# Softmax factors of three chunks spread by VectorE instead of by DMA, and a fold ahead of an accumulate, in a fused attention and expert kernel

## The chip, the cores and the metric

The kernel runs on one core of a Trainium2 chip. The metric is the device time of one execution in microseconds (us). PE is TensorE, DVE is VectorE, ACT is ScalarE, POOL is GpSimd, and SP is the engine that issues most DMAs. A `q` behind a name (SPq, POOLq) is that engine's instruction queue.

## The reference

For one sequence of S = 2048 tokens and D = 1024 channels, two branches over the same input are mixed by a gate. Their core:

```python
qkv = (x @ wqkv).reshape(B, S, 3, 32, 32).transpose(2, 0, 3, 1, 4)
scores = einsum("bhqd,bhkd->bhqk", q, k) * 32 ** -0.5
o = einsum("bhqk,bhkd->bhqd", softmax(scores), v)
a = o.transpose(0, 2, 1, 3).reshape(B, S, D) @ wo
# b: per head h a top-1 choice out of 64 experts, out = sum_h gelu(x . u[e]) * v[e]
g = sigmoid((x * gate_w).sum(-1))
out = g * a + (1 - g) * b
```

The change concerns attention's last stage alone: the row sums of the softmax and the product with `wo`.

## The kernel before, in words

**Attention.** The 32 heads run one after the other, each over NT = 16 key tiles of 128. For a tile, TensorE computes scores (L1292), ScalarE exponentiates them into a tile `P[h, kt]` of 128x2048 (L1301), and TensorE multiplies them with the values into `o` (L1313). The softmax is not normalized there. Its denominators, the sums of `P` over keys, are gathered beside it: VectorE adds the tiles of a head into `ACC[h]` (`presum`, `add_pair`, `merge`, all through `add`, L1353, two instructions of 128x1024 for a tile), and some pairs of tiles are first added by DMAs that accumulate, issued by POOL (`accumulate`, L1342). `pairs_of(h)` names the pairs as (target, source). For the last head, 31, they are (2, 4) and (2, 6): both add into `P[31, 2]`.

**Row sums.** For most heads, DMAs on POOL's queue fold `ACC[h]` from 128 partitions to 64 and to 32 (`fold`, L1361), store them (`store_rows`, tensors `sed`), and later fold these in DRAM. For the last group (heads 28 to 31) TensorE does the end of it: head 30's `ACC` is folded to 64 partitions, `rows_back` (L1373) loads the stored rows of heads 28 and 29 into its other half, and `rowsums` (L1326) multiplies head 31's last two tiles, `ACC[31]` and `ACC[30]` by ones. `norm_sums` copies the sums out (ScalarE, tile `ssb`) and stores them in `smd`; `load_r` reads them back as `rr`, `norm_r` takes VectorE's reciprocals, and the result goes to the tensor `rd`: one factor for each head and token.

**What sets the order there.** A dictionary `todo` of steps, one step for a key tile. `at(step, f, ...)` puts a call in a step; the calls of one step run in the order in which the loop over heads entered them. Each engine's queue runs in program order. An issued DMA waits for the landing of the eighth one before it that was issued on the same side (POOL, or SP and ACT), as they share eight semaphores.

**Output.** The result is computed in eight chunks of W = 256 tokens. For chunk n, `load_o` loads `OC[n]` (tile `V`, eight DMAs of 128x256 from the tensors `od`) and `load_rb` the factors `RB[n]`: a factor belongs to a head, which is 32 partitions of `OC`, so a row of `rd` is loaded 32 times, once into each of the 32 partitions, by a DMA whose source repeats. Four such DMAs (j = 0 to 3) make a chunk. VectorE multiplies `OC[n]` by `RB[n]` in two halves of 128x1024. Chunks 0 and 1 go through `split_o` (each operand split into a high and a low part, L1627) and plain matmuls (`wo_mm`, L1559, three products of 128x512 for a block); `av_mm` (L1566) adds the expert branch with the operand `at`. Chunks 2 to 7 go through `scale_o` (L1612) and a Strassen scheme: `ht.operand(...)` forms A11, S3, S1 and so on from `OC[n]`, `ht.product("P1")` and so on runs twelve matmuls each (L155). The last head's group (kc = 7) can be normalized only when the row sums are there; so chunks 0 and 1 load their rows 0 to 6 ahead and row 7 later. `RB[0]` lies in `rb0`, and `RB[n]` in a tile `P8` or `P9`.

TensorE runs `wo_mm` of chunk 0 over kc 0 to 6, `av_mm` of chunk 0, `wo_mm` of chunk 1 over 1, 2, 3 and 0, then chunk 0's kc 7, chunk 1's kc 4 to 6, `av_mm` of chunk 1 and its kc 7, and then chunk 2's P1, P7, P5, P6 and so on.

## Time and profile before

| | |
|---|---|
| median of 3 runs | 1811.92 us (1811.81 to 1812.72) |
| profiled execution | 1813.99 us, its span 1812.2 us |
| PE busy | 1798.1 us, 99% of the span |
| DVE busy | 1495.0 us, 82% |
| ACT busy | 1216.4 us, 67% |
| POOL busy | 281.6 us, 16% |
| granted TensorE clock, mean | 0.998 |
| DMA | 362.19 MB, mean 200 GB/s |

The span is the time from the first to the last instruction of one profiled execution. Busy times of different engines overlap. In the 14 us in which PE isn't busy lie its start and the end of the kernel too. The attention stage ends near 1620 us of the span, and the output stage fills the rest.

### The profile page before, as it was taken

What the parts mean: (1) busy time and instruction counts of PE and PEld (TensorE: products, weight loads), DVE (VectorE), ACT (ScalarE), POOL (GpSimd) and SP (SyncE); (2) the same over time, 40 slices, a digit from 0 to 9 for tenths busy, and PEclk for the clock granted to TensorE, in tenths of its full rate; (3) what the DMA queues carried; (4) which work ended last, traced back from release to release, by engine and by line L of the source; (5) the groups of instructions that cost most, each with busy time, mean ns of one, the idle gap of its engine ahead of it and who ended that gap; (6) DMA issues with size and microseconds to landing.
All of it is one profiled execution on the core that took longest, in us unless ns stands there. A gap on an engine that the chain in (4) does not pass through costs nothing.

```text
span 1812.2 us, 27968 instructions
## 1 busy us (share of the span) xinstructions
PE 1798.1 (99%) x10559; PEld 1136.5 (63%) x10559; DVE 1495.0 (82%) x1673; ACT 1216.4 (67%) x1604; POOL 281.6 (16%) x351
## 2 busy tenths in 40 slices
PE   9999999999999999999999999999999999999899
PEld 7877777788888745554555545455555455448787
DVE  6868776358987689899899899999989989893684
ACT  4434321211233399999999999999999999982221
POOL 0212000026401211111111111111121111221000
PEclk9999999999999999999999999999999999999999
DMA  6887889823238688899899998998999998977861
GB/s 234 242 283 241 273 272 292 262 79 106 82 130 273 228 199 182 175 187 193 185 207 188 208 195 181 193 211 193 198 216 200 207 214 189 203 172 183 283 177 59
DMA packets 132050, 362.19 MB, mean 200 GB/s; under 512 B 18676, under 2 KB 57732, under 8 KB 106360
## 3 DMA queue, kind: packets, MB, share of 16 engines
q0 software_dynamic: 22736, 134.89, 36.6%
q1 hardware_dynamic: 89016, 189.56, 36.1%
q10 hardware_dynamic: 20160, 35.92, 7.0%
q8 instruction: 84, 1.38, 0.3%
q14 instruction: 54, 0.44, 0.1%
HBM read 176.77 MB, written 86.61 MB: 145 GB/s over the span
## 4 chain that ended last, share of the span: by engine, by line
PE 90%; DMA 4%; ACT 2%; DVE 1%; SPq 1%; issue 1%; POOL 0%; ACTq 0%; DVEq 0%; POOLq 0%
PE ring L1292 27%; PE o L1313 25%; PE bk L155 11%; PE bk L711 9%; PE pa L155 6%; PE bk L758 5%; PE bk L926 2%; PE bk L311 2%; PE bk L491 1%; ACT P L1301 1%; SPq L82 1%; DMA wraw<-in_wqkv 1%; DMA V<-od 1%; PE bk L395 1%; PE pa L1566 1%
## 5 line engine op out<-in xcount | busy, mean ns | idle before, releaser
L1301 ACT ACTIVATE P<-ring 128x512 f32<-128x512 f32 (+3 forms) x986 | 808.1, 942 | 14.0 <-PE ring L1292 8.5
L1353 DVE TENSOR_TENSOR acc<-acc,P 128x1024 f32<-128x1024 f32 x408 | 469.4, 1215 | 22.1 <-ACT P L1301 22.1
L1313 PE MATMUL o<-P,V 128*32 128x512 f32 (+1 forms) x4040 | 412.6, 529 | 0.0
L1292 PE MATMUL ring<-Q,K 98*128 98x512 f32 x1024 | 268.5, 406 | 0.1
L1292 PE MATMUL ring<-z,z 98*128 98x512 f32 x1020 | 267.6, 406 | 0.1
L1292 PEld LDWEIGHTS ring<-Q,K 98*128 98x128 f32 x1024 | 182.6, 188 | 116.8 <-ACT P L1301 38.6
L1292 PEld LDWEIGHTS ring<-z,z 98*128 98x128 f32 x1020 | 182.1, 188 | 114.6 <-issue 37.8
L1313 PEld LDWEIGHTS o<-P,V 128*32 128x32 f32 x4040 | 111.6, 109 | 218.2 <-issue 198.4
L1353 DVE TENSOR_TENSOR rb<-rb,P 128x1024 f32<-128x1024 f32 x186 | 214.3, 1215 | 5.6 <-ACT P L1301 5.6
L1342 POOL DMA_DIRECT2D P<-P x60 | 55.7, 928 | 362.9 <-PE o L1313 141.8
L240 ACT ACTIVATE hi<-bk 128x512 fp32r<-128x512 f32 x40 | 23.7, 595 | 111.5 <-PE bk L711 94.7
L1301 ACT ACTIVATE wo_raw<-ring 128x512 f32<-128x512 f32 (+3 forms) x115 | 97.5, 942 | 0.7
L711 PE MATMUL bk<-xh,e 128*128 128x512 f32 x384 | 94.5, 394 | 0.2 <-DVE e L101 0.2
L711 PE MATMUL bk<-xl,e 128*128 128x512 f32 x384 | 92.2, 389 | 0.0
L711 PEld LDWEIGHTS bk<-xh,e 128*128 128x128 f32 x384 | 70.9, 188 | 22.5 <-issue 3.4
L711 PEld LDWEIGHTS bk<-xl,e 128*128 128x128 f32 x384 | 72.1, 188 | 15.0
L253 DVE TENSOR_TENSOR lo<-bk,hi 128x512 fp32r<-128x512 f32 x40 | 27.6, 689 | 64.8 <-ACT hi L240 59.7
L101 DVE TENSOR_TENSOR e<-wraw,e 128x512 fp32r<-128x512 f32 (+3 forms) x64 | 54.3, 858 | 29.7 <-ACT e L100 29.0
L1301 ACT ACTIVATE vhl<-ring 128x512 f32<-128x512 f32 (+3 forms) x89 | 76.9, 939 | 0.9 <-PE ring L1292 0.2
L100 ACT ACTIVATE e<-wraw 128x512 fp32r<-128x512 f32 (+3 forms) x64 | 44.7, 705 | 42.6 <-DMA wraw<-in_wqkv 26.1
L1353 DVE TENSOR_TENSOR acc<-acc,wo_raw 128x1024 f32<-128x1024 f32 x60 | 70.1, 1216 | 1.8 <-ACT wo_raw L1301 1.8
L155 PE MATMUL bk<-xh,e 128*128 128x512 f32 x288 | 68.6, 393 | 0.0
(305 smaller groups left out, 2454.7 us busy)
## 6 DMA issues: line engine op xcount, KB each, us to landing
P<-P POOLq DMA_DIRECT2D x60, 1024.0 KB, 10.2
wqt<-in_wq SPq DMA_DIRECT2D x26, 1024.0 KB
wraw<-in_wqkv SPq DMA_DIRECT2D x30, 512.0 KB
acc<-acc POOLq DMA_DIRECT2D x21, 512.0 KB, 6.6
qdh<-hi ACTq DMA_DIRECT2D x32, 256.0 KB
qdl<-lo ACTq DMA_DIRECT2D x32, 256.0 KB
kdh<-hi ACTq DMA_DIRECT2D x32, 256.0 KB
kdl<-lo ACTq DMA_DIRECT2D x32, 256.0 KB
```

The lines of the kernel that those rows point to most:

```text
L100: nc.scalar.activation(hi, src, AF.Copy)
L101: (on or nc.vector).tensor_tensor(out=lo, in0=src, in1=hi.bitcast(F32), op=OP.subtract)
L155: nc.tensor.matmul(ps, self.a[a][i][:, k, :], self.b[b][j][k], start=(not first and k == 0 and i == j == 0), stop=(k == HC - 1 and i == 1))
L311: nc.tensor.matmul(ps[32 * quad:32 * quad + 32, :], kpad[:, quad % 2, i, :], t[:, quad, :], start=(i == 0), stop=(i == 3))
L711: nc.tensor.matmul(ps, t[:, kc // HC, a, kc % HC], x_at(b, n, kc), start=first, stop=last)
L758: nc.tensor.matmul(ps, x_at(a, t // 4, kc)[:, tok], b, start=first, stop=last)
L926: nc.tensor.matmul(p, x_at(a, t // 4, kc)[:, tok], b, start=first, stop=last)
L1292: on_ring(nc.tensor.matmul(ring[:, i, :], K[:98, kt * 128:(kt + 1) * 128], Q[:98, qc * 512:(qc + 1) * 512], start=True, stop=True), i)
L1301: on_ring(nc.scalar.activation(P[h, kt][:, q0 * 512:(q0 + m) * 512].rearrange("p (a m) -> p a m", a=m), ring[:, i:i + m, :], AF.Exp, scale ...
L1313: nc.tensor.matmul(O[h][32 * qc:32 * qc + 32, c0:c1], Vt[g][:, kt, 32 * j:32 * j + 32], p[:, qc * 512 + c0:qc * 512 + c1], start=(kt == 0) ...
L1342: nc.gpsimd.dma_start(P[h, b], P[h, a], accum_op=OP.add)
L1353: nc.vector.tensor_add(out[:, c], a[:, c], b[:, c])
```

## The change

Four edits, all at the end of attention and in the output stage.

1. `norm_sums` stores the four heads' sums with one DMA of 16 rows instead of four DMAs of 4 rows.
2. An `accumulate` runs at step a + 2 instead of b + 4. For every pair with a = b + 2 that is the same step. Only head 31's second pair, (2, 6), moves, by two steps, and comes behind the fold of head 30, which was entered in that step before it.
3. For chunks 1 to 3, `load_rb` loads a row into the first of its 32 partitions only. POOL sets the tile to zero first (`memset`, 128x2048), and `factors` has VectorE's shuffle copy partition 0 of each 32 to all 32, in place, ahead of each product. Chunk 3 reuses chunk 1's tile.
4. In the program's order, rows 0 to 6 of chunk 1's factors come ahead of its `V` loads, those of chunk 2 right behind them (on POOL's queue, before on SP's), and chunk 3's factors move from POOL's queue to SP's, behind chunk 0's output.

```diff
     def norm_sums(ps):
...
-        for j in range(4):
-            dma(SMD[G - 1][j:j + 1, :].rearrange("o (q s) -> (o q) s", q=NQ), o[8 * j::32, :])
+        dma(SMD[G - 1].rearrange("j (q s) -> q j s", q=NQ), o[::8, :])
...
+    SHUFFLED = 1, 2, 3
...
     def load_rb(n, k0, k1, js=range(4), queue=nc.sync):
-        if n not in RB:
+        if n == 3:
+            RB[n] = RB[1]
+        elif n not in RB:
             RB[n] = rb0 if n == 0 else wk.tile([128, KC, W], F32, name=f"P{8 + n % 2}", bufs=1)
+            if n in SHUFFLED:
+                nc.gpsimd.memset(RB[n], 0.0)
+        rows = 1 if n in SHUFFLED else 32
         for j in js:
             src = RD[k0:k1, j:j + 1, n * W:(n + 1) * W].rearrange("g j s -> j g s")
-            dma(RB[n][32 * j:32 * j + 32, k0:k1, :], src.to_broadcast([32, k1 - k0, W]), queue)
+            dma(RB[n][32 * j:32 * j + rows, k0:k1, :], src.to_broadcast([rows, k1 - k0, W]), queue)
+
+    def factors(n, k0, k1):
+        r = RB[n][:, k0:k1, :]
+        if n in SHUFFLED:
+            flat = r.rearrange("p k m -> p (k m)")
+            nc.vector.stream_shuffle(flat, flat, [0] * 32)
+        return r
...
         for b, a in pairs_of(h):
-            at(base + b + 4, accumulate, h, b, a)
+            at(base + a + 2, accumulate, h, b, a)
...
         for k in range(2):
             o = OC[n][:, k * HC:(k + 1) * HC]
-            nc.vector.tensor_mul(o, o, RB[n][:, k * HC:(k + 1) * HC])
+            nc.vector.tensor_mul(o, o, factors(n, k * HC, (k + 1) * HC))
...
     def split_o(n, k0, k1):
         o = OC[n][:, k0:k1, :]
-        nc.vector.tensor_mul(o, o, RB[n][:, k0:k1, :])
+        nc.vector.tensor_mul(o, o, factors(n, k0, k1))
...
-    load_chunk(1, 0, KC - 1, nc.gpsimd)
+    load_rb(1, 0, KC - 1, queue=nc.gpsimd)
+    load_o(1, 0, KC - 1, nc.gpsimd)
+    load_rb(2, 0, KC - 1, queue=nc.gpsimd)
...
-    load_rb(2, 0, KC)
+    load_rb(2, KC - 1, KC)
     load_o(2, 0, KC)
...
     split_o(1, HC, KC)
-    load_rb(3, 0, KC, queue=nc.gpsimd)
     load_at(2)
...
     plain_out(0, pa, nc.gpsimd)
+    load_rb(3, 0, KC)
     load_o(3, 0, KC)
```

What that does to the queues is best seen in three places. First POOL's queue around head 30's fold, before the change. `P_12653` is `P[31, 2]`, `P_12687` and `P_12722` are its two sources, `acc<-acc` is head 30's fold, `acc<-sed` the two loads of `rows_back`, and `V` is chunk 1's:

```order
L1342 DMA P_12653<-P_12687 128x2048
L1342 DMA P_12653<-P_12722 128x2048
L1361 DMA acc<-acc 64x2048
L1373 DMA acc<-sed_95 32x2048 x2
L82 DMA V<-od_71 128x256
```

After the change, with `P_12961` for the factors of chunk 1:

```order
L1342 DMA P_12653<-P_12687 128x2048
L1361 DMA acc<-acc 64x2048
L1342 DMA P_12653<-P_12722 128x2048
L1373 DMA acc<-sed_95 32x2048 x2
L1421 MEMSET P_12961 128x2048
L82 DMA P_12961<-rd 1x7x256 x4
L82 DMA V<-od_71 128x256
```

The fold has passed the second accumulate, and a memset and four loads of a few rows stand ahead of `V`. Second, further down in POOL's queue, from chunk 1's last `V` load to the stores of chunk 0, before (`P_12969` are chunk 1's factors, `P_13216` chunk 3's):

```order
L82 DMA V<-od_77 128x256
L82 DMA P_12969<-rd 32x7x256 x4
L82 DMA at<-atd 128x256 x2
L82 DMA P_13216<-rd 32x8x256 x4
L82 DMA out<-rb_5214 128x512 x4
```

And after (`P_12975` are chunk 2's):

```order
L82 DMA V<-od_77 128x256
L1421 MEMSET P_12975 128x2048
L82 DMA P_12975<-rd 1x7x256 x4
L82 DMA at<-atd 128x256 x2
L82 DMA out<-rb_5214 128x512 x4
```

A second memset stands ahead of `at`, and chunk 3's factors have left the queue. Third, VectorE from the reciprocals to chunk 2's operands, before (`V<-V,P` are the products with the factors, `rr` the row sums, `pa` the results of chunk 0):

```order
L1402 RECIPROCAL rr<-rr 128x64
L1403 TENSOR_TENSOR rr<-rr,G_110 128x64
L1627 TENSOR_TENSOR V<-V,P_12969 128x1024
L101 TENSOR_TENSOR acc<-V,z_13110 128x1024
L1627 TENSOR_TENSOR V<-V,rb_5214 128x256
L101 TENSOR_TENSOR acc<-V,z_12763 128x256
L1627 TENSOR_TENSOR V<-V,P_12969 128x1024
L101 TENSOR_TENSOR acc<-V,z_13110 128x1024
L1622 COPY rb_5214<-pa_12922 128x512
L1622 COPY rb_5214<-pa_12924 128x512
L1612 TENSOR_TENSOR V<-V,P_13115 128x1024 x2
```

And after:

```order
L1402 TENSOR_TENSOR rr<-rr,G_110 128x64
L1431 STREAM_SHUFFLE P_12961<-P_12961 128x1024
L1639 TENSOR_TENSOR V<-V,P_12961 128x1024
L101 TENSOR_TENSOR acc<-V,z_13114 128x1024
L1639 TENSOR_TENSOR V<-V,rb_5214 128x256
L101 TENSOR_TENSOR acc<-V,z_12762 128x256
L1431 STREAM_SHUFFLE P_12961<-P_12961 128x1024
L1639 TENSOR_TENSOR V<-V,P_12961 128x1024
L101 TENSOR_TENSOR acc<-V,z_13114 128x1024
L1634 COPY rb_5214<-pa_12922 128x512
L1634 COPY rb_5214<-pa_12924 128x512
L1431 STREAM_SHUFFLE P_12975<-P_12975 128x1024
```

Each product with the factors of chunks 1 to 3 has a shuffle right ahead of it. TensorE's and ScalarE's own sequences are the same as before.

## The prediction

> **What bounds the kernel now.** I read the engine totals first, then the stages, then TensorE's own timeline, and only then the chain of waits. TensorE is busy nearly throughout (the table above), so the only time to be had is where it stands still or runs slowly. The timeline of TensorE's instructions from 1600 us on (start, busy time, line, count, idle time before with its releaser in brackets) shows two such places:

> ```profile
> 1624.88 2.07 PE L1326 MATMUL o<-acc,ones 128*32 128x512 f32 x8
> 1629.05 1.06 PE L1326 MATMUL o<-acc,ones 128*32 128x512 f32 x8 [2.09 <-DMA acc<-sed]
> 1630.05 2.05 PE L1559 MATMUL pa<-woh,z 128*128 128x512 f32 x4
> ...
> 1634.49 1.07 PE L1559 MATMUL pa<-woh,z 128*128 128x512 f32 x4
> ...
> 1648.09 1.98 PE L1566 MATMUL pa<-vhl,at 128*128 128x512 f32 x8
> ...
> 1675.29 1.07 PE L1559 MATMUL pa<-woh,acc 128*128 128x512 f32 x4
> 1681.10 0.64 PE L155 MATMUL pa<-woh,acc 128*128 128x512 f32 x1 [4.74 <-ACT acc L100]
> ...
> 1685.85 0.40 PE L155 MATMUL pa<-z,s 128*128 128x512 f32 x1
> ```

> Gap A: the row sums of head 30 wait 2.09 us for `rows_back`. Gap B: the first Strassen product of chunk 2 waits 4.74 us for its operand A11. Each gap has a tail in which TensorE runs at about half clock. The table of stages (length, busy time of PE, PEld, DVE, ACT, POOL, then granted clock, DMA share, GB/s) shows the clock after each gap, and that nothing like it follows:

> ```profile
> 1630.00:1632.00 2.00, 2.00 (x9) 1.57 (x6) 0.68 (x3) 1.81 (x4) 1.70 (x3) 0.53 0.99 403
> 1682.00:1684.00 2.00, 1.82 (x5) 1.36 (x5) 1.30 (x3) 0.63 (x1) 0.00 (x0) 0.50 0.98 409
> 1690.00:1812.00 122.00, 118.43 (x523) 97.73 (x521) 79.14 (x118) 25.05 (x42) 0.00 (x0) 1.00 0.54 152
> ```

> From 1690 us the 122.00 us hold 118.43 us of matmul, and the rest is the final store: whatever brings TensorE earlier to 1690 us brings the end earlier by as much.

> What the gaps are worth: at full clock twelve wide matmuls take 2.72 us (four start every 0.907 us). From 1630.05 to 1634.49 there are twelve, which took 4.44, so gap A costs 2.09 + 1.72 = 3.81 us. Gap B starts where the last four should end, 1675.29 + 0.91 = 1676.20; the product starts at 1681.10 (4.90 later) and its twelve matmuls last until 1685.85 (4.75, 2.03 too long): 6.93 us. Both together are 10.74 us, the most that this change can bring.

> [...]

> **The fold ahead of the second pair.** POOL's queue and the chain of waits behind it:

> ```profile
> 1598.61 0.90 POOL L1342 DMA_DIRECT2D P<-P  x1 [4.28 <-ACT P L1301]
> 1609.07 0.88 POOL L1342 DMA_DIRECT2D P<-P  x1 [9.56 <-ACT P L1301]
> 1609.62 1.18 POOL L1361 DMA_DIRECT2D acc<-acc  x1
> 1622.47 0.51 POOL L1373 DMA_DIRECT2D acc<-sed  x1 [1.39 <-DMA rb<-rd]
> 1632.83 0.59 POOL L82 DMA_DIRECT2D at<-atd  x1 [0.90 <-DMA V<-od]
> ```
> ```profile
> 1609.62 10.66 DMA acc<-acc
> 1622.47 6.54 DMA acc<-sed
> 1632.43 10.06 DMA smd<-ssb
> 1670.15 10.29 DMA V<-od
> ```
> ```profile
> 1595.74 9.16 DVE L1353 TENSOR_TENSOR acc<-acc,P 128x1024 f32<-128x1024 f32 x8
> 1604.82 0.41 DVE L1441 TENSOR_TENSOR V<-V,ssb 128x256 f32<-128x256 f32 x1
> 1616.69 9.16 DVE L1353 TENSOR_TENSOR acc<-acc,P 128x1024 f32<-128x1024 f32 x8
> 1679.16 2.54 DVE L1612 TENSOR_TENSOR V<-V,P 128x1024 f32<-128x1024 f32 x2 [14.84 <-DMA V<-od]
> ```

> The second accumulate adds into the same tile as the first, so it can't go before the first has landed; the ScalarE named there had long written the tile. The fold stands behind it although its own input, head 30's merge, is the last of the eight additions that end at 1604.82. Ahead of it, the fold goes at about 1604.9 instead of 1609.62, 4.7 us earlier. With the same 10.66 and 6.54 us to landing, `rows_back` lands at 1629.01 - 4.7 = 1624.3. Late next is head 31's own sum: its additions end at 1616.69 + 9.16 = 1625.85, and TensorE is through with them at 1626.95. So 2.7 us are to spare and gap A goes whole. The accumulate put behind loses nothing, as it waits for the first one's landing anyway; with the fold's 10.66 us to landing it ends at 1619.7, and VectorE's third addition, which reads it, is due at 1616.69 + 2 x 2.29 = 1621.27.

> **The loads, the shuffles, the one store.** Sizes per DMA and time to landing (KB each, us), then three lines of the timelines of ScalarE and SP:

> ```profile
> P<-rd SPq DMA_DIRECT2D x4, 256.0 KB
> P<-rd POOLq DMA_DIRECT2D x4, 256.0 KB, 13.6
> P<-rd POOLq DMA_DIRECT2D x4, 224.0 KB, 8.9
> V<-od POOLq DMA_DIRECT2D x7, 128.0 KB, 7.1
> out<-rb POOLq DMA_DIRECT2D x4, 256.0 KB, 13.1
> 1647.00 1.06 ACT L100 ACTIVATE z<-V 128x1024 fp32r<-128x1024 f32 x1 [9.18 <-DVE V L1627]
> 1630.81 2.10 SPq L82 DMA_DIRECT2D smd<-ssb  x4
> 1657.84 13.37 SPq L82 DMA_DIRECT2D V<-od  x8
> ```

> The factors of chunks 1 to 3 are 0.9 + 1 + 1 MB, and become a thirty-second of that. Three 0.5 us issues of `smd` fall away (1.6 us). So the chain row sums, `smd`, `rr`, reciprocal, `rd` moves by at least 2.1 + 1.6 = 3.7 us, and by more if `smd`'s 10.06 us shrink, since the 0.9 MB of chunk 1 were moving just then. In it stands one new shuffle. TensorE needs the operand behind it after the eight matmuls of 1648.09, at 1649.9 - 3.81 = 1646.1. ScalarE's half of it ended at 1648.06, so 1648.06 - 3.7 + 1.2 = 1645.6: no wait even without any gain in the DMA.

> Gap B hangs on chunk 2's eight `V<-od`: issued from 1657.84, landed at 1670.15 + 10.29 = 1680.44, 22.6 us for 1 MB, with 2 MB of factors (SP's ahead of them, POOL's beside) and 1 MB of stores in flight. TensorE will be ready at 1676.20 - 3.81 = 1672.4. The products and A11's rounding took 1681.10 - 1680.44 = 0.7 us past the landing and the low half 1.9, so the data must land by 1670.4. Bounds: nothing gained, 22.6 us, lands at 1657.84 - 3.7 + 1.2 + 22.6 = 1677.9; issue at 0.4 us each and the 6.54 us of `rows_back`, about 10, lands at 1665. Without 2 of 4 MB I take the half, 11.3 us: 1666.6, nearly 4 us to spare. One third less is enough to hide it all. Gap B goes whole.

> The shuffle is not in this trace. Nearest is the product of the same 128x1024 form, 2.54/2 = 1.27 us; the dearest VectorE form is this reciprocal:

> ```profile
> 1644.95 0.55 DVE L1402 RECIPROCAL rr<-rr 128x64 f32<-128x64 f32 x1 [4.28 <-DMA rr<-smd]
> L1812 POOL MEMSET const-float32-0.0<- 128x1 f32 x1 | 0.1, 100 | 0.3 <-issue 0.3
> L137 POOL TENSOR_TENSOR wraw<-wraw,wraw 128x512 f32<-128x512 f32 x5 | 8.1, 1616 | 0.4
> DMA to landing us min/median/max: 8.2/8.4/8.7
> ```

> At its pace 1024 columns would be 8.8 us, the upper end; no gain is possible, as each is one more instruction. I take 1.2, six of them, 7.2 us. [...] Chunk 1's two are covered above, chunk 2's by the 4 us to spare (the first needs no `V`), chunk 3's two by VectorE being busy 79.14 of 122.00 us while TensorE holds eight banks of products. Uncovered they would cost 2.5 us a chunk. Chunk 3's factors move from POOL to SP ahead of its `V` loads, four small issues whose reader is one product group later: nothing.

> The two memsets of 128x2048 stand in POOL's queue ahead of chunk 1's loads and of `at`, TensorE's operand at 1648.09 - 3.81 = 1644.3. Bounds: 0.1 us (a 128x1 memset) and 4 x 1.62 = 6.5 us (adding two inputs); one written, none read, I take 2.6. The first waits for the second accumulate and `rows_back`, about 1619. Fifteen issues of 0.59 us follow before `at` goes, at 1619 + 8.9 + 5.2 = 1633.1, about as now (1632.83). Each issue also waits for the landing of the eighth before it, `at` for the fourth `V`: that one goes at 1619 + 2.6 + 8 x 0.59 = 1626.3 and lands 7.1 later, 1633.4, which is no more. `at` lands 8.4 later at 1641.8. With 2.5 us to spare, memsets up to 3.8 us cost nothing.

> **The sum.** 3.81 + 6.93 = 10.74 us off the profiled execution, 1813.99 - 10.74 = 1803.25. The median of the runs, 1811.92, is 2.07 under that execution. If the 2.07 lay outside the gaps the median becomes 1801.2; if they lay within the gaps, 1803.2. I take the middle, 1802.2.

> **The rivals.**
> *Only gap A goes.* `V` of chunk 2 lands at 1677.9 at worst, five and a half us after TensorE is ready, and gap B stays as long as it was: 1811.92 - 3.8 = 1808.1. For it: each `V` issue waits for an earlier landing, and 1 MB of stores stays. Against: two thirds of what went before and beside them is gone. Chance of this or something between it and the forecast 0.13, spread over 1803.4 to 1808.

> *Only gap B goes.* The early fold shares the DMA engines with the first accumulate, or `rows_back` with the second, and 2.7 us to spare are eaten: 1811.92 - 6.9 = 1805.0. Against: the same bytes in the same stretch. Chance 0.06.

> *The change doesn't do what it says*: the waits move on to the same length (a `T` block or `rr` late instead), 1811 to 1812. Chance 0.03.

> *Slower: the memset.* If a memset of 2048 columns takes far longer than an addition does, chunk 1's loads and `at` are late. At 6.5 us each `at` goes at 1640.9 and lands at 1649.3, 5.0 after need; with 1.7 us at half clock that is 1811.92 - 10.74 + 6.7 = 1807.9. It turns slower where the wait passes 10.74 - 1.7 = 9.0 us, at 8.5 us a memset; at 10.5 us each the wait is 13.0 and the time 1811.92 + 13.0 + 1.7 - 10.74 = 1815.9. For it: no memset of that size is in the trace. [...] Chance 0.04.

> **The numbers.** The forecast, both gaps gone, has 0.74; its own range is 1801.0 to 1803.4. The range down to 1800.8 and up to 1806.5 takes in case B and half of the between cases, 0.87, of which some is left for what I have not seen. About 0.2%, 3.6 us, is what a measurement of this kernel tells from no change: under 1808.3 lie the forecast, both partial cases and half of the milder memset, 0.92; the rest is 0.04 the same and 0.04 slower.

> **What would show it.** Right: POOL's fold at about 1605; the row sums of head 30 without idle time; no clock under 1.00 after 1600; `smd` landing earlier than 1642; `V<-od` of chunk 2 issued in about 4 us rather than 13.37; six shuffles near 1.2 us. Wrong: an idle time of TensorE before L1326, before `at`, before chunk 1's `woh,z` or before L155, and the name of its releaser says which term failed.

## The result, and the profile after

The changed kernel takes 1802.05 us in the median of 6 runs (1800.88 to 1802.37), the kernel before, run beside it, 1812.32 us in the median of 6 (1810.1 to 1813.31). The ratio is 0.9943, with a 95% interval of 0.993 to 0.9956: faster by 0.57%, about 10.3 us. The profiled execution took 1801.88 us, its span is 1800.1 us.

TensorE's timeline after the change (start, busy time, line, count) at the two places; the helper's lines have moved by 12, so L1559 reads L1571:

```profile
1623.76 2.88 PE L1326 MATMUL o<-acc,ones 128*32 128x512 f32 x16
1626.57 1.20 PE L1571 MATMUL pa<-woh,z 128*128 128x512 f32 x4
1629.42 1.07 PE L1571 MATMUL pa<-woh,z 128*128 128x512 f32 x4
...
1670.22 1.07 PE L1571 MATMUL pa<-woh,acc 128*128 128x512 f32 x4
1671.12 0.39 PE L155 MATMUL pa<-woh,acc 128*128 128x512 f32 x1
1673.84 0.39 PE L155 MATMUL pa<-z,s 128*128 128x512 f32 x1
```

No row has a bracket: `ACC[31]` and `ACC[30]` are one run of 16 matmuls, and chunk 2's P1 follows the last `wo_mm` at once. The table of stages says the same of the clock (the column after POOL's):

```profile
1626.00:1628.00 2.00, 2.00 (x10) 1.22 (x7) 2.00 (x4) 2.00 (x4) 2.00 (x3) 1.00 0.92 336
1630.00:1632.00 2.00, 2.00 (x11) 1.65 (x10) 2.00 (x5) 1.94 (x3) 1.84 (x4) 1.00 0.29 107
1674.00:1676.00 2.00, 2.00 (x11) 1.65 (x10) 0.00 (x0) 1.96 (x4) 0.00 (x0) 1.00 0.68 177
```

Where the time came from is read off equal places of the two traces. Chunk 0's second group of `wo_mm` started at 1634.49 and now starts at 1629.42, 5.07 us earlier. TensorE was 1.12 us earlier already when it reached `ACC[31]` (1624.88, now 1623.76), which leaves 3.95 us for gap A. P7 of chunk 2 started at 1685.85 and now at 1673.84, 12.01 us earlier, so gap B gave another 6.94. Behind it nothing is won or lost: the span is 12.1 us shorter. I put the 1.12 us down to the two profiled executions and not to the change: the other eleven traces below get there between 1622.92 and 1624.03, among them `fold_only`, the kernel before but for one line, at 1623.28.

POOL's queue, with the fold (L1361) now between the two accumulates (L1342), then one row each of VectorE and SP:

```profile
1604.02 0.83 POOL L1361 DMA_DIRECT2D acc<-acc  x1 [5.63 <-DVE acc L1353]
1608.46 0.90 POOL L1342 DMA_DIRECT2D P<-P  x1 [3.62 <-ACT P L1301]
1612.07 0.51 POOL L1373 DMA_DIRECT2D acc<-sed  x1 [1.38 <-issue]
1616.63 1.81 POOL L1421 MEMSET P<- 128x2048 f32 x1 [4.05 <-PE o L1313]
1626.59 1.84 POOL L1421 MEMSET P<- 128x2048 f32 x1
1630.71 1.18 POOL L82 DMA_DIRECT2D at<-atd  x2
```
```profile
1638.52 1.33 DVE L1431 STREAM_SHUFFLE P<-P 128x1024 f32<-128x1024 f32 x1
1664.21 0.68 DVE L101 TENSOR_TENSOR acc<-V,acc 128x512 fp32r<-128x512 f32 x1
1627.31 0.51 SPq L82 DMA_DIRECT2D smd<-ssb  x1
1633.44 0.34 SPq L82 DMA_DIRECT2D rr<-smd  x1
1647.75 3.67 SPq L82 DMA_DIRECT2D V<-od  x8
```

The sizes and times to landing of the DMAs between 1590 and 1700 us (KB each, us):

```profile
acc<-acc POOLq DMA_DIRECT2D x1, 512.0 KB, 5.8
acc<-sed POOLq DMA_DIRECT2D x2, 256.0 KB, 8.8
at<-atd POOLq DMA_DIRECT2D x2, 128.0 KB, 3.3
```

The fold lands after 5.8 us instead of 10.66, `at` after 3.3 instead of 8.4, and chunk 2's eight `V` loads are issued in 3.67 us instead of 13.37. From the issue of `smd` to the issue of `rr` behind its landing pass 6.1 us; before it was 1630.81 to 1642.98, 12.2 us.

### The profile page after: what moved, and what is told of

Its sections match the earlier page's. It is cut to its first block, busy times and chain, and to the rows that moved or that the text cites. A ratio compares the mean times of both kernels' runs of the same rounds, so it can differ in the third digit from the quotient of the medians.

```text
span 1800.1 us, 27993 instructions
## 1 busy us (share of the span) xinstructions
PE 1793.7 (100%) x10559; PEld 1135.3 (63%) x10559; DVE 1502.7 (83%) x1685; ACT 1216.7 (68%) x1604; POOL 284.0 (16%) x353
## 4 chain that ended last, share of the span: by engine, by line
PE 98%; DMA 1%; ACT 0%; SPq 0%; issue 0%; DVE 0%; ACTq 0%; DVEq 0%
PE ring L1292 28%; PE o L1313 26%; PE bk L155 13%; PE bk L711 10%; PE pa L155 6%; PE bk L758 5%; PE pa L1571 2%; PE bk L926 2%; PE bk L311 2%; PE bk L491 1%; PE pa L1578 1%; PE bk L395 1%; DMA wraw<-in_wqkv 1%; ACT P L1301 0%; SPq L82 0%; PE o L1326 0%
## 5 line engine op out<-in xcount | busy, mean ns | idle before, releaser
L1301 ACT ACTIVATE P<-ring 128x512 f32<-128x512 f32 (+3 forms) x986 | 808.1, 942 | 14.0 <-PE ring L1292 8.6
L1353 DVE TENSOR_TENSOR acc<-acc,P 128x1024 f32<-128x1024 f32 x408 | 469.7, 1219 | 22.1 <-ACT P L1301 22.1
L1353 DVE TENSOR_TENSOR rb<-rb,P 128x1024 f32<-128x1024 f32 x186 | 214.4, 1219 | 5.6 <-ACT P L1301 5.6
L1342 POOL DMA_DIRECT2D P<-P x60 | 55.7, 928 | 354.6 <-PE o L1313 141.1
L1301 ACT ACTIVATE wo_raw<-ring 128x512 f32<-128x512 f32 (+3 forms) x115 | 97.6, 942 | 0.6
L711 PE MATMUL bk<-xh,e 128*128 128x512 f32 x384 | 94.2, 394 | 0.0
L1301 ACT ACTIVATE vhl<-ring 128x512 f32<-128x512 f32 (+3 forms) x89 | 76.9, 940 | 0.9 <-PE ring L1292 0.2
L1353 DVE TENSOR_TENSOR acc<-acc,wo_raw 128x1024 f32<-128x1024 f32 x60 | 70.2, 1219 | 1.8 <-ACT wo_raw L1301 1.8
L100 ACT ACTIVATE e<-wraw 128x512 fp32r<-128x512 f32 (+3 forms) x64 | 44.6, 705 | 36.8 <-DMA wraw<-in_wqkv 16.2
L1361 POOL DMA_DIRECT2D acc<-acc x41 | 33.7, 822 | 221.0 <-DMA acc<-acc 83.3
## 6 DMA issues: line engine op xcount, KB each, us to landing
P<-P POOLq DMA_DIRECT2D x60, 1024.0 KB, 10.3
qdh<-hi ACTq DMA_DIRECT2D x32, 256.0 KB
qdl<-lo ACTq DMA_DIRECT2D x32, 256.0 KB
kdh<-hi ACTq DMA_DIRECT2D x32, 256.0 KB
kdl<-lo ACTq DMA_DIRECT2D x32, 256.0 KB
```

Source lines behind the costliest of these rows:

```text
L100: nc.scalar.activation(hi, src, AF.Copy)
L711: nc.tensor.matmul(ps, t[:, kc // HC, a, kc % HC], x_at(b, n, kc), start=first, stop=last)
L1301: on_ring(nc.scalar.activation(P[h, kt][:, q0 * 512:(q0 + m) * 512].rearrange("p (a m) -> p a m", a=m), ring[:, i:i + m, :], AF.Exp, scale ...
L1342: nc.gpsimd.dma_start(P[h, b], P[h, a], accum_op=OP.add)
L1353: nc.vector.tensor_add(out[:, c], a[:, c], b[:, c])
```

## The experiments

Theory: gap A goes by the fold's place in POOL's queue alone, gap B by the bytes of the factors that no longer move, and shuffles and memsets are hidden. Rivals: it is the order of the loads, or the single store, that does it; or shuffles and memsets are near to costing.

### One half at a time

`fold_only` is the kernel before with edit 2 alone:

```diff
-            at(base + b + 4, accumulate, h, b, a)
+            at(base + a + 2, accumulate, h, b, a)
```

> The kernel before, with the accumulate at step a + 2 alone, so that head 30's fold passes head 31's second pair. Theory: gap A goes (3.8 us), but chunk 2's V loads move earlier only as far as the chain from the row sums to rd moves, 2 us or somewhat more, so the wait before the first Strassen product (L155) grows from 4.7 to about 6.5 us and the gain is 2 to 4 us: 1808 to 1810. Rival, the two gains simply add: the wait before L155 stays 4.7 us and the time is 3.8 less, 1808.5, with V landing 3.8 us earlier.

Measured: 1809.45 us (1808.15 to 1811.99, 11 runs) beside 1812.29 us, ratio 0.9982 [0.9973, 0.9991]. Gap A is gone, and part of what it gave is lost again in gap B. TensorE's row before P1 and SP's `V` loads in this trace:

```profile
1676.72 0.79 PE L155 MATMUL pa<-woh,acc 128*128 128x512 f32 x1 [5.51 <-ACT acc L100]
1653.93 12.70 SPq L82 DMA_DIRECT2D V<-od  x8
```

TensorE is at P1 earlier, chunk 2's data not as much, so it waits 5.51 us instead of 4.74. The issue of the `V` loads still takes 12.70 us. The time alone doesn't tell the theory from the rival, whose 1808.5 lies within the interval. The wait does, as far as one trace can: the two gaps' prices do not simply add when only one goes.

`loads_only` is the changed kernel with that line put back:

```diff
-            at(base + a + 2, accumulate, h, b, a)
+            at(base + b + 4, accumulate, h, b, a)
```

> The changed kernel with the accumulate back at step b + 4. Theory: gap A returns whole (2.1 us of idle time before the row sums of head 30 and 1.7 us at half clock), no idle time before L155: 1802.05 + 3.8 = 1805.9. Rival, the lighter DMA traffic lets rows_back land earlier by itself: gap A under 1 us and 1803 or less.

Measured: 1804.21 us in the median of 5 runs (1803.0 to 1808.26), ratio 0.996 [0.9946, 0.9974]. Gap B is gone, gap A is back, but with no loss of clock behind it:

```profile
1627.87 1.06 PE L1326 MATMUL o<-acc,ones 128*32 128x512 f32 x8 [2.46 <-DMA acc<-sed]
1628.87 1.20 PE L1571 MATMUL pa<-woh,z 128*128 128x512 f32 x4
```

The four matmuls take 1.20 us here; after the 2.09 us of the kernel before they took 2.05. The runs spread over 5 us, too (the changed kernel's six lie within 1.5). So the same file was profiled twice more.

> The kernel of the loads_only run once more: its row sums waited 2.46 us and its clock stayed at 1.00, while the kernel before waited 2.09 us in the same place and fell to 0.53. Theory: whether an idle time of 2 to 2.5 us costs clock is a matter of how it lies to a window that runs free of the program, so the same program sometimes loses 1.7 us more and sometimes not. Then the idle time before L1326 is again 2 to 3 us, and the clock of 1630 to 1634 may be 1.00 or near 0.5; the time is 1803 to 1804.5 with the clock kept and 1805 to 1807 without it. Rival: the clock depends on the program (what lies beside the gap), and is 1.00 again in every profile of this kernel.

> The same kernel a third time, with the same expectation: idle time of 2 to 3 us before L1326, clock 1.00 or near 0.5 behind it by the window theory, 1.00 by the rival.

Measured: 1808.23 and 1807.2 us, beside 1812.98 us. The same rows, of `loads_b` and then of `loads_c`:

```profile
1629.24 1.94 PE L1326 MATMUL o<-acc,ones 128*32 128x512 f32 x8 [3.45 <-DMA acc<-sed]
1631.10 2.08 PE L1571 MATMUL pa<-woh,z 128*128 128x512 f32 x4
```
```profile
1627.94 1.93 PE L1326 MATMUL o<-acc,ones 128*32 128x512 f32 x8 [2.80 <-DMA acc<-sed]
1629.80 2.08 PE L1571 MATMUL pa<-woh,z 128*128 128x512 f32 x4
```

One program, three profiles: after 2.46 us of idle time the clock is kept (1.00 from 1628 to 1634 us), after 2.80 and 3.45 it is halved (0.50 from 1630 to 1634 us in both). The rival, that the program alone decides it, is out. The length of the gap alone doesn't decide it either, as 2.09 us were enough in the kernel before (0.53 from 1630 to 1632 us). Gaps and times were longer than expected, by up to 0.45 and 1.2 us. Over all seven runs, on two chips, `loads_only` takes 1805.8 us in the mean, 3.8 above the changed kernel, and none lies between 1804.21 and 1806.48: gap A costs 1.0 to 2.2 us in three of them and 4.4 to 6.2 in four.

### Bytes, order, or the store

`order_only`: the changed kernel with every factor loaded 32 times, as before, but in the new order.

```diff
-    SHUFFLED = 1, 2, 3
+    SHUFFLED = ()
```

> The changed kernel, but all chunks load their factors 32 times as before (no memset, no shuffle): the new order of loads, the single store and the fold ahead are kept. Theory, the bytes count: 0.9 MB more for chunk 1 and 0.9 MB for chunk 2 stand in POOL's queue ahead of at, which lands late, and 1 MB for chunk 3 stands on SP; TensorE waits before L1578 or L155 by 2 us or more: 1805 to 1811. Rival, moving chunk 2's factors ahead and chunk 3's behind is what closes gap B: 1802.

Measured: 1809.17 us (1807.03 to 1810.66, 11 runs), ratio 0.9982 [0.9973, 0.9991]. The time is as expected, the place is not: before `at` (L1578) TensorE waits 0.28 us and before P1 (L155) not at all; the wait is at chunk 1's operand. SP's `smd`, `rr` and chunk 2's `V` loads, then TensorE at chunk 1's operand and at P1:

```profile
1627.56 0.51 SPq L82 DMA_DIRECT2D smd<-ssb  x1
1644.63 0.34 SPq L82 DMA_DIRECT2D rr<-smd  x1
1659.34 3.69 SPq L82 DMA_DIRECT2D V<-od  x8
1649.74 2.08 PE L1571 MATMUL pa<-woh,z 128*128 128x512 f32 x4 [3.91 <-ACT z L100]
1679.06 0.39 PE L155 MATMUL pa<-woh,acc 128*128 128x512 f32 x1
```

The same 32 KB store, issued at the same time as in the changed kernel, takes 17.1 us until `rr` can go, instead of 6.1. POOL's queue then held eight 224 KB loads of factors in place of eight of 7 KB. So what was late is the whole chain of row sums, behind the loads of the factors.

The rival is right about gap B itself, though not about the time. With every factor still loaded 32 times, the new order lets chunk 2's `V` loads be issued in 3.69 us instead of 13.37, and A11 is ready at 1670.05, sooner even than the changed kernel asks for it (1671.12). In this trace the order, with the single store, closes gap B without fewer bytes, but what it gains there is lost again in front of chunk 1's operand: the 1809.17 us are no better than the 1809.45 of `fold_only`.

By bytes I mean the repeated loads as a whole; their bytes, their packets and their place in POOL's queue were not separated. It need not be the bytes: from 1636 to 1640 us the DMA engines were busy for 0.90 of the time in this trace and moved 158 GB/s, and in the changed kernel's for 1.00 and moved 406, with other loads in flight.

`bytes_only`: the changed kernel with the loads in the order of before (edit 4 undone).

```diff
-    load_rb(1, 0, KC - 1, queue=nc.gpsimd)
-    load_o(1, 0, KC - 1, nc.gpsimd)
-    load_rb(2, 0, KC - 1, queue=nc.gpsimd)
+    load_chunk(1, 0, KC - 1, nc.gpsimd)
...
-    load_rb(2, KC - 1, KC)
+    load_rb(2, 0, KC)
...
+    load_rb(3, 0, KC, queue=nc.gpsimd)
...
-    load_rb(3, 0, KC)
```

> The changed kernel with the loads in the order of the kernel before (chunk 1's V ahead of its factors, chunk 2's factors all on SP ahead of its V, chunk 3's on POOL), but each factor row loaded once and shuffled. Theory: the bytes are what gap B hangs on, so no idle time before L155: 1802. Rival, the order matters as well: the wait before L155 keeps 1 us or more, 1803.5 or over.

Measured: 1801.98 us (1801.56 to 1802.19), ratio 0.9941 [0.9927, 0.9955]. With the repeated loads gone, the order adds nothing that can be measured. Fewer bytes suffice for all that gap B is worth; the order alone, by the run above, gives no time.

`four_stores`: the changed kernel with four DMAs for `smd` again (edit 1 undone).

```diff
-        dma(SMD[G - 1].rearrange("j (q s) -> q j s", q=NQ), o[::8, :])
+        for j in range(4):
+            dma(SMD[G - 1][j:j + 1, :].rearrange("o (q s) -> (o q) s", q=NQ), o[8 * j::32, :])
```

> The changed kernel with norm_sums storing by four DMAs again. Theory: the chain from smd to chunk 1's operand is 1.6 us longer, and TensorE needs that operand 2.8 us after it is ready, so nothing changes: 1802 within 0.3. Rival, the chain is on the path: 1803.6 and an idle time before chunk 1's first product (L1571).

Measured: 1801.9 us (1801.59 to 1802.21), ratio 0.9939 [0.9926, 0.9953]. The single store is worth nothing either.

### The two added costs, multiplied

`memset4` and `memset6` write each of the two tiles four and six times:

```diff
-                nc.gpsimd.memset(RB[n], 0.0)
+                for _ in range(4):
+                    nc.gpsimd.memset(RB[n], 0.0)
```

> The changed kernel with each of the two memsets issued four times (7.3 us instead of 1.8 each). Theory: at goes at 1630.7 + 11.0 = 1641.7 and lands 3.3 us later, 1645, against TensorE's need at 1643.2: an idle time of 1 to 2.4 us before L1578 and, if so short a gap drops the clock as gap A did, 1.7 us more: 1803 to 1806. Rival, POOL's memset also holds up VectorE's additions: L1353 longer than 1.22 us and head 31's sums late, 1808 or more.

Measured: 1803.31 us (1802.22 to 1806.65). At 7.42 us for the four, `at` is issued at 1640.58 instead of 1630.71, and in the profiled run TensorE waits for it for a quarter of a microsecond:

```profile
1640.58 1.12 POOL L82 DMA_DIRECT2D at<-atd  x2
1643.19 2.11 PE L1579 MATMUL pa<-vhl,at 128*128 128x512 f32 x8 [0.26 <-DMA at<-atd]
```

This is the fastest of the four runs. The others took 1802.39, 1804.23 and 1806.65 us; they have no trace, so how long TensorE waited there is not known.

> The changed kernel with each memset issued six times (11 us each). Theory: at goes 18.4 us later, lands near 1652 and TensorE waits 9 us before L1578, with 1.7 us at half clock behind it, of which nothing is made up later: 1813. Rival, slack behind L1578 takes some of it, as chunk 2 is ready early: under 1810.

Measured: 1811.29 us (1810.3 to 1812.29), ratio 0.9993 [0.9984, 1.0003]: all of the gain is gone. The time lies between the theory's 1813 and the rival's 1810. The wait is 7.55 us rather than 9, and the matmuls after it run at half clock (0.50 from 1651 to 1655 us; the eight take 3.78 us, where the changed kernel's take 1.98):

```profile
1650.77 3.78 PE L1579 MATMUL pa<-vhl,at 128*128 128x512 f32 x8 [7.55 <-DMA at<-atd]
```

VectorE's additions, which run beside the first of these memsets, take as long as ever. The durations of L1353 between 1590 and 1660 us (ns, least, median, most), of `memset6` and of the kernel before:

```profile
L1353 DVE TENSOR_TENSOR acc<-acc,P x27: 1211/1214/1221, 1588.9 to 1623.5; 128x1024 f32<-128x1024 f32 x27
```
```profile
L1353 DVE TENSOR_TENSOR acc<-acc,P x28: 1211/1215/1220, 1588.9 to 1624.6; 128x1024 f32<-128x1024 f32 x28
```

None of the 27 of `memset6`, those beside its first memsets (1617.29 to 1628.45 us) among them, takes longer than 1221 ns, and the longest of the kernel before takes 1220. So POOL's memset doesn't hold up these additions.

`shuffle3` and `shuffle2` issue each shuffle three times and twice:

```diff
-            nc.vector.stream_shuffle(flat, flat, [0] * 32)
+            for _ in range(3):
+                nc.vector.stream_shuffle(flat, flat, [0] * 32)
```

> The changed kernel with each shuffle issued three times (4.0 us instead of 1.35). Theory: TensorE has 2.8 us to spare at chunk 1's first operand and about 6 at chunk 2's, so 2.7 more in the first and 5.4 more in the second just fit: 1802 to 1803. Rival, the shuffles are on the path: 12 more of 1.35 us give up to 16 us, 1818.

Measured: 1805.46 us (1805.0 to 1805.8), ratio 0.9959 [0.9944, 0.9974]. The expectation missed, and by a chunk that it did not name. VectorE's subtraction, which forms the low part of A11, and TensorE's wait, which that ends:

```profile
1691.41 0.68 DVE L101 TENSOR_TENSOR acc<-V,acc 128x512 fp32r<-128x512 f32 x1
1692.15 0.73 PE L155 MATMUL pa<-woh,acc 128*128 128x512 f32 x2 [2.47 <-DVE acc L101]
```

This is A11 of chunk 3, not of chunk 2: six shuffles of chunk 3 stand ahead of it in VectorE's queue.

> Each shuffle issued twice. In the changed kernel chunk 3's first operand is rounded by 1685.15 us and TensorE asks for it near 1689.5; with three shuffles it came at 1692.09. Theory: chunk 3's two extra shuffles add 2.7 us, and those of chunk 2 push VectorE by another 0.8, so the operand comes at about 1688.7 and no wait is left: 1801.5 to 1802.5. Rival: VectorE has no room at all in that stretch, and the time rises in proportion, by half of the 3.5 us that three shuffles cost: 1803.5 to 1804.

Measured: 1801.39 us (1800.97 to 1802.05), beside 1812.98 us, ratio 0.994 [0.9923, 0.9956], and TensorE waits for nothing from 1590 us on. In this trace the low part of chunk 3's A11 is formed at

```profile
1686.36 0.68 DVE L101 TENSOR_TENSOR acc<-V,acc 128x512 fp32r<-128x512 f32 x1
```

So chunk 3's pair has room for one more shuffle each (2.7 us) and not for two (5.4 us). The changed kernel's own trace puts the room at about 4 us (ready by 1685.15, asked for near 1689).

## Why the prediction was right, step by step

**The sum.** The terms were 3.81 + 6.93; equal places of the traces give 3.95 + 6.94. The forecast of 1802.2 met 1802.05. The choice between 1801.2 and 1803.2, whether the 2.07 us by which the profiled execution was slow lay inside the gaps, was left to a middle; by the trace the profiled executions differ upstream too (1.12 us), so there was no better ground for it than that. That the middle met the median within 0.15 us is luck: the price of gap A alone changes by some us from run to run, and the kernel before's median moved from 1811.92 to 1812.32 when three runs became six. One slip of addition: the chances of the cases under 1808.3 add up to 0.93 and more, where the prediction has 0.92.

**Gap A.** Right in mechanism: the fold goes at 1604.02 (1604.9 said). The terms behind it were off. I carried over 10.66 us to landing for the fold and 6.54 for `rows_back`; measured are 5.8 for the fold, and 7.8 and 9.7 for the two loads of `rows_back` (8.8 above is their median). So `rows_back` lands at 1612.07 + 9.7 = 1621.8 and not 1624.3. The fold lands faster because of its place in the queue, not because of the lighter loads: it takes 5.0 to 6.1 us in all nine traces in which it goes ahead of the second accumulate, `fold_only` among them, and 10.5 to 10.7 in the four in which it goes behind. A 1 MB accumulate was issued half a microsecond ahead of it before; whether that alone is the reason wasn't tested. The term that the runs correct is the 1.72 us of half clock: that is what one profile had. With the gap back in place one profile of `loads_only` lost nothing behind it, and the other two ran at half clock for 6.3 and 5.7 us of matmuls, a loss of about 3 us.

**Gap B.** Right: fewer bytes close it, as `bytes_only` shows. The prediction didn't see that the new order alone would close it too, as `order_only` shows; what the fewer bytes add is that no wait comes up at chunk 1's operand in its place. What I sized as half of 22.6 us, landing at 1666.6, is better: with the issues done at 1647.75 + 3.67 = 1651.4, VectorE multiplies without waiting for data, and A11 is ready at 1664.21 + 0.68 = 1664.9, 6.2 us before P1. The 1.6 us credited to the three issues of `smd` saved were worth nothing by themselves; the gain in that chain is the store's landing.

**Shuffles.** 1.33 to 1.37 us each against 1.2. The cover of chunks 1 and 2 held; the argument for chunk 3, VectorE busy 79.14 of 122.00 us, was too loose. A share over 122 us says nothing of the 4 us in which one operand is due.

**Memsets.** 1.81 and 1.84 us against 2.6. "Memsets up to 3.8 us each cost nothing" was probably too careful: at 7.42 us the wait is 0.26 in the one profiled run, where `at` lands in 3.0 us and not 8.4. But the four runs lie 0.2 to 4.6 us above the changed kernel's median, so 7.42 us is no longer free, and where the cost begins wasn't measured. The point at which the change would turn slower, said to be 8.5 us a memset, lies near the 11.2 us of `memset6`.

**The partial cases** were priced at 1808.1 (only A) and 1805.0 (only B). Built, they take 1809.45 and 1805.8 in the mean of seven runs, the first more because gap B grows when A goes.

## What the runs showed of the clock

The stretches at half clock are whole multiples of 3.41 us. The granted clock of a microsecond is 1.00 or 0.50 in the stages read from these traces, and between them only at the start and the end of such a stretch; so the value there tells where in the microsecond the change fell. The stages of 1 us at the start and end of such stretches, first the two of the kernel before:

```profile
1630.00:1631.00 1.00, 1.00 (x6) 0.81 (x3) 0.44 (x2) 0.81 (x2) 1.00 (x2) 0.55 0.95 393
1633.00:1634.00 1.00, 1.00 (x4) 0.79 (x4) 1.00 (x3) 1.00 (x2) 0.64 (x2) 0.74 0.92 205
1681.00:1682.00 1.00, 0.90 (x2) 0.34 (x2) 1.00 (x2) 0.05 (x1) 0.00 (x0) 0.65 1.11 467
1684.00:1685.00 1.00, 1.00 (x5) 0.76 (x4) 0.89 (x2) 0.08 (x1) 0.00 (x0) 0.64 1.01 395
```

A clock of 0.55 is full for a tenth of the microsecond and half for the rest, so it fell at 1630.10; it rose at 1633.52, fell at 1681.30 and rose at 1684.72. Both stretches last 3.42 us, and 51.20 us lie between the two falls, 15 times 3.413. The same for `loads_c` and for `memset6`:

```profile
1627.00:1628.00 1.00, 0.06 (x4) 0.06 (x8) 1.00 (x4) 0.34 (x2) 0.37 (x1) 0.72 0.88 311
1634.00:1635.00 1.00, 1.00 (x6) 0.77 (x5) 1.00 (x3) 1.00 (x2) 0.80 (x2) 0.87 0.12 45
```
```profile
1645.00:1646.00 1.00, 0.00 (x0) 0.00 (x0) 0.00 (x0) 0.00 (x0) 0.71 (x2) 0.82 0.23 71
1655.00:1656.00 1.00, 1.00 (x4) 0.77 (x4) 0.00 (x0) 0.00 (x0) 0.00 (x0) 0.56 0.87 287
```

They last 6.82 and 10.24 us, two and three times 3.41; those of `loads_b`, `order_only` and `fold_only` last 6.82, 6.82 and 6.84. The clock of the kernel before falls once more at its end, at 1811.00 (1.00 in the microsecond before, 0.50 in the one from there), 180.90 us behind its first fall: 53 times 3.413. The falls have no fixed place in the program: `loads_b` and `loads_c` are one program, and theirs are at 1628.16 and 1627.44, 0.72 us apart. Nor do they come a fixed time after the idle time begins: 2.30 us after it in `loads_c`, 3.15 in gap A of the kernel before, 4.94 in its gap B.

## What to carry to other kernels

In these traces a short wait of the engine that bounds the kernel had a price with two values: its own length (2.46 us in the profile of `loads_only`, with the clock at 1.00), or that and some microseconds of half clock (2.09 us of wait and 1.72 more in the kernel before, 2.80 and 3.45 and about 3 more in `loads_c` and `loads_b`); read it from several profiles, and take the wait away rather than trim it. Loads that repeat a source over 32 partitions held up a small transfer that mattered more: 1.8 MB of them on one queue held a 32 KB store, on which the next stage hung, by 11 us (17.1 against 6.1), and one row with a 1.35 us shuffle in their place removed that. A new order of the loads closed one wait (4.74 us before P1) and opened another (3.91 us at chunk 1's operand), so look for where the wait has gone. Check the cover of an added instruction at the one operand that it delays, between the time it is ready and the time it is asked for; doubling and tripling the instruction brackets the true room in two runs, here between 2.7 and 5.4 us.
